# Averages of two blocks and the first dense rows turned by VectorE through DRAM, in a two-layer attention and Mish kernel

## The chip, the cores and the metric

The kernel runs on one core of a Trainium2 chip. The metric is the device time of one execution in microseconds; lower is better. The core has TensorE (PE, matrix products into PSUM), VectorE (DVE), ScalarE (ACT), GpSimd (POOL) and SyncE (SP, which issues all DMAs of this kernel in one queue).

## The reference

Two layers of the same kind over x of 2048 rows and 640 columns, all in 32 bit. Each layer is linear attention with a learned feature map, then a dense Mish block, both with a layer norm before and a residual after. The weights are the same in both layers.

```python
# attention: H = 32 heads of 20
q, k, v = heads of layernorm(x) @ wqkv
pq, pk  = q @ w_phi, k @ w_phi                     # per head
phi     = concat(softmax(p), softmax(-p))          # for q and for k, 40 features
kv, z   = phi_k^T v, sum over rows of phi_k
o       = (phi_q kv) / (phi_q z + 1e-6)            # "averages"
x       = x + o @ wo
# dense
h       = layernorm(x) @ w1 + b1                   # 640 -> 1536
x       = x + (h * tanh(softplus(h))) @ w2         # 1536 -> 640
```

## The kernel before, in words

Rows are worked on in 8 blocks (b = 0 to 7, NB = 8) of 256 rows, each of BT = 2 tiles (t = 0, 1) of 128 rows. Every large product is made of three products: an operand is split into a high part that TensorE's fast form takes, and the low rest (`xth` and `xtl` for activations, `r1h`, `r1l`, `r2h`, `r2l` for weights), and high x high, high x low and low x high are added up in PSUM.

The left operand of a product has to lie with its columns on the partitions. Rows are turned for that in one of two ways, both in the class `Transposed`:

- With `rows`: TensorE transposes 128x128 pieces against the identity (L280), ten for a block, into PSUM tiles named `one`; ScalarE copies out the high part (`xth`, recorded at L116 since all calls of the helper `act` have that line), and VectorE subtracts for the low part (`xtl`, L286).
- With `cols`: VectorE has turned the rows in 32x32 blocks (L315, `spill_turned`), eight DMAs have stored them to DRAM so that the blocks come to lie in the right place (L317, runs of 32 numbers), and `load_turned` (L325) has loaded them; `xth` and `xtl` are then made from that tile in SBUF. The dense layer uses this for its blocks 1 to 7 (`n1_d`), and the second layer's attention for its input (`n2_d`).

A layer has three stages.

1. `attend_first` makes q, k and v, the features, and the sum kv; the query features go to DRAM, turned (`e_d`).
2. `attend_second` runs over the 8 blocks. `load` (`phi`) brings the features of a block; `average` makes its averages on TensorE (L573) and VectorE divides them into a row tile `xn` (L582 to L586); they are transposed; the output projection (L344) runs in halves of 320 columns (`Rows.half`); VectorE adds the half to x in place (L603), takes the statistics (L604, L608), GpSimd makes the scale from them (L259, L260) and VectorE the shift (L262); x is stored to `x1_d` (L669). Between the blocks the dense weights are fetched (L141) and split (L148, L149, and L116). The averages run ahead of the projection: block b + 2 is averaged in the middle of block b, and block b + 1 is transposed just before it. The first dense block's rows are made in this stage as well: block 0 of `x1_d` is loaded (`fetch_dense`, L852), normalized by ScalarE (`normed`), and transposed on TensorE at the start of block 7 (`ahead.all()`, L639).
3. `dense` runs over the 8 blocks, with the first product at L695, Mish on ScalarE, VectorE and GpSimd, and the second product at L737.

What sets the order: in `attend_second` TensorE and SyncE run in exactly the order in which the code calls them (`tc.manual_schedule` on PE and SP). VectorE, ScalarE and GpSimd are ordered when the program is built, by a planner with a model of the times; afterwards each engine runs its instructions strictly in that order. A DMA with a wait holds up all DMAs behind it on SyncE's queue. Buffers come from pools of fixed counts: `big` has five tiles of 128x1280, `xn` four row tiles, `x` two blocks, and PSUM has four `one` and two `mm` tiles.

Of the kernel before, what the change touches and what calls it, by code (L numbers as in the profile page):

```python
# [8 lines left out]
F32 = mybir.dt.float32  # L9
# [33 lines left out]
def kernel(  # L43
# [58 lines left out]

    n1_d = [dram.tile([D, BLK], F32, name=f"n1_d{b}") for b in range(NB)]
    n2_d = [dram.tile([D, BLK], F32, name=f"n2_d{b}") for b in range(NB)]
    x1_d = dram.tile([S, D], F32, name="x1_d")
    x2_d = dram.tile([S, D], F32, name="x2_d")

# [157 lines left out]
    class Transposed:  # L265
# [5 lines left out]
        def step(self):  # L271
            c0 = len(self.hs)
            n = min(2, KD - c0)
            if self.rows is None:
                ps = self.cols[c0 // 2]
            else:
                ps = one_tile().rearrange("p (c s) -> p c s", c=2)
                for c in range(n):
                    for t in range(BT):
                        nc.tensor.transpose(ps[:, c, t * P:(t + 1) * P],  # L280
                                            self.rows[t][:, (c0 + c) * P:(c0 + c + 1) * P], ident)
            nb = 8 if n == 2 else 4
            hi = work.tile([P, n, BLK], F32R, tag=f"xt{n}", name="xth", bufs=nb)
            lo = work.tile([P, n, BLK], F32R, tag=f"xt{n}", name="xtl", bufs=nb)
            act(hi, ps[:, :n], AF.Copy)
            nc.vector.tensor_tensor(lo, ps[:, :n], hi.bitcast(F32), op=ALU.subtract)  # L286
            for c in range(n):
                self.hs.append(hi[:, c, :])
                self.ls.append(lo[:, c, :])
# [29 lines left out]
    def load_turned(src, tiles):  # L319

        cols = []
        for c, make in zip(range(0, KD, 2), tiles):
            n = min(2, KD - c)
            cols.append(make()[:, :n * BLK].rearrange("p (k s) -> p k s", k=n))
            nc.sync.dma_start(cols[-1], src[c * P:(c + n) * P].rearrange("(k p) s -> p k s", p=P))  # L325
        return Transposed(cols=cols)


    def project(xts, t, ws, col, ps=None):
# [220 lines left out]
                nc.vector.tensor_copy(kvb[:80, 5, :42], ps[:80, 1, :42])  # L550
        yield

    def attend_second(x_src, x_dst, acc, fetches, makes, fetch_next, begin_next):
        kva, kvz, o_ws, loaded, rest = acc
        rows = {}
        div = [None]
# [54 lines left out]
        with tc.manual_schedule(engines={mybir.EngineType.PE, mybir.EngineType.SP}):  # L611
# [21 lines left out]
            def phi(b):  # L633
                if b < NB:
                    loaded[b] = load(b)

            for b in range(NB):
                if b == NB - 1:
                    ahead.all()  # L639
# [2 lines left out]
                r0, r1 = Rows(b, 0), Rows(b, 1)  # L642
                r0.half(0, one_tile())
                tail()
                if b + 1 < NB:
                    xs[b + 1] = fetch(x_src, b + 1)
                if b in (1, 2):
                    phi(b + 3)
                if b == NB - 3:
                    fetch_next()  # L650
                r0.half(1, one_tile())
                mv0 = r0.mean()
                if b == NB - 2:
# [12 lines left out]
                r1.half(1, one_tile())  # L666
                norm_scale(b, [mv0, r1.mean()])
                xt = xs.pop(b)
                nc.sync.dma_start(row_block(x_dst, b), xt)  # L669
                makes[b]()  # L670
# [145 lines left out]
    with tc.block(schedule_with_timeline_sim=True):  # L816
        src, first = x, None
        for layer in range(LAYERS):
# [38 lines left out]
            begun = attend_second(src, x1_d, acc, [lambda s=s: fetch_step(*s) for s in steps],  # L857
                                  [lambda s=s: make_step(*s) for s in steps], fetch_dense, begin_dense)
            first = dense(x1_d, dst, w1s, w2s, [x1t[0], begun, None], last)
            src = dst  # L860

# [37 lines left out]
```

## Time and profile before

| | |
|---|---|
| time, median of 3 runs | 1398.45 us (1397.73 to 1398.70) |
| the profiled execution | 1396.09 us, its span 1394.3 us |
| TensorE busy | 1380.7 us, 99% of the span |
| VectorE / ScalarE / GpSimd busy | 1075.5 us (77%) / 583.3 us (42%) / 440.0 us (32%) |
| mean granted TensorE clock | 0.999 |
| HBM traffic | 120 GB/s over the span |

The span runs from the first to the last instruction. A row of the timeline has the start, the length, the engine, the line in the kernel, the operation, and output <- inputs by tile names (buffer numbers are left out); x10 means that ten instructions in a row are put together; a bracket names how long the engine sat idle ahead of it and what it waited for. A row of the groups has busy time, mean ns of one, and idle time before. A row of waits reads: engine, tile and line <- what it waited for: us in total, times, longest. A row of DMA issues has the count, the size and the median time from issue to landing. SPq is SyncE's queue, and its rows show how long the issue of a DMA took, not the transfer.

### The profile page before, as it was taken

How to read it: one execution, taken by the hardware profiler on the slowest of the kernel's cores; microseconds unless marked ns; L12 is line 12 of the kernel's file. 1: busy time of each engine (PE TensorE's matmuls, PEld its weight loads, DVE VectorE, ACT ScalarE, POOL GpSimd, SP SyncE). 2: the span in 40 equal slices, each digit the busy share in tenths (PEclk: the TensorE clock that was granted, in tenths of full speed). 3: DMA queues.
4: the chain of work that ended last, by engine and by line, in shares of the span. 5: the costliest groups of instructions: out<-in, count | busy, mean ns of one | idle time of the engine just before them, and what ended most of it. 6: DMA issues, size and time to landing. Idle time of an engine off the chain costs nothing. (4 is left out here: it accounts for less than half of the span.)

```text
span 1394.3 us, 28137 instructions
## 1 busy us (share of the span) xinstructions
PE 1380.7 (99%) x11528; PEld 1367.0 (98%) x11528; DVE 1075.5 (77%) x1820; ACT 583.3 (42%) x973; POOL 440.0 (32%) x334
## 2 busy tenths in 40 slices
PE   7999999999999999999999999999999999999998
PEld 7999999999999999999999999999999999999998
DVE  5797877796698877788769988888767876777775
ACT  4444433321355454545454333332235444444443
POOL 1353443343422221222234434343342211211112
PEclk9999999999999999999999999999999999999999
DMA  8533333689633432343474333357976212333200
GB/s 328 162 79 54 67 52 58 184 228 307 235 86 95 114 84 62 83 114 95 122 261 87 71 57 58 65 107 231 288 257 200 76 25 72 95 95 95 75 22 20
DMA packets 350035, 169.57 MB, mean 122 GB/s; under 512 B 286866, under 2 KB 323458, under 8 KB 349906
## 3 DMA queue, kind: packets, MB, share of 16 engines
q1 hardware_dynamic: 349906, 167.78, 44.2%
q8 instruction: 90, 1.47, 0.4%
q14 instruction: 39, 0.32, 0.1%
HBM read 104.82 MB, written 62.91 MB: 120 GB/s over the span
## 5 line engine op out<-in xcount | busy, mean ns | idle before, releaser
L737 PE MATMUL mm<-r2h,ol 128*128 128x320 f32 x1280 | 304.7, 309 | 0.0
L721 POOL TENSOR_TENSOR ol<-big,ol 128x512 fp32r<-128x512 f32 (+1 forms) x98 | 129.8, 1324 | 483.5 <-ACT ol L720 407.3
L695 PE MATMUL one<-xtl,r1h 128*128 128x256 f32 x960 | 268.2, 279 | 0.0
L695 PE MATMUL one<-xth,r1l 128*128 128x256 f32 x960 | 268.0, 279 | 0.0
L695 PE MATMUL one<-xth,r1h 128*128 128x256 f32 x960 | 265.9, 279 | 0.0
L737 PEld LDWEIGHTS mm<-r2h,ol 128*128 128x128 f32 x1280 | 219.1, 188 | 0.0
L737 PE MATMUL mm<-r2l,ol 128*128 128x320 f32 x640 | 197.3, 309 | 0.0
L344 PE MATMUL mm<-r1h,xth 128*128 128x320 f32 x600 | 187.3, 312 | 0.0
L344 PE MATMUL mm<-r1h,xtl 128*128 128x320 f32 x600 | 186.0, 310 | 0.7 <-DVE xtl L286 0.7
L344 PE MATMUL mm<-r1l,xth 128*128 128x320 f32 x600 | 186.0, 310 | 0.0
L695 PEld LDWEIGHTS one<-xtl,r1h 128*128 128x128 f32 x960 | 180.4, 188 | 0.0
L695 PEld LDWEIGHTS one<-xth,r1l 128*128 128x128 f32 x960 | 180.4, 188 | 0.0
L695 PEld LDWEIGHTS one<-xth,r1h 128*128 128x128 f32 x960 | 179.6, 188 | 0.0
L710 DVE TENSOR_SCALAR big<-big 128x512 f32<-128x512 f32 (+1 forms) x98 | 57.1, 583 | 109.9 <-ACT big L708 109.7
L379 POOL TENSOR_TENSOR r<-r,r 128x1280 f32<-128x1280 f32 x32 | 75.8, 2368 | 163.1 <-DVE r L378 157.3
L737 PEld LDWEIGHTS mm<-r2l,ol 128*128 128x128 f32 x640 | 120.2, 188 | 0.0
L712 ACT ACTIVATE big<-big,two 128x512 f32<-128x512 f32 (+1 forms) x98 | 70.1, 715 | 116.2 <-DVE big L711 116.1
L708 ACT ACTIVATE big<-one,b1s 128x256 f32<-128x256 f32 x192 | 80.8, 467 | 90.1 <-PE one L695 89.6
L720 ACT ACTIVATE ol<-big 128x512 fp32r<-128x512 f32 (+1 forms) x98 | 61.0, 622 | 136.0 <-DVE big L719 135.9
L344 PEld LDWEIGHTS mm<-r1h,xth 128*128 128x128 f32 x600 | 112.8, 188 | 1.3
L344 PEld LDWEIGHTS mm<-r1h,xtl 128*128 128x128 f32 x600 | 112.7, 188 | 1.3 <-DVE xtl L286 1.0
L344 PEld LDWEIGHTS mm<-r1l,xth 128*128 128x128 f32 x600 | 112.8, 188 | 0.1
(129 smaller groups left out, 3156.1 us busy)
## 6 DMA issues: line engine op xcount, KB each, us to landing
e_d<-r SPq DMA_DIRECT2D x128, 160.0 KB, 4.0
big<-e_d SPq DMA_DIRECT2D x32, 640.0 KB, 6.6
x_d<-xt SPq DMA_DIRECT2D x23, 640.0 KB, 3.9
xt<-x_d SPq DMA_DIRECT2D x22, 640.0 KB, 4.3
n_d<-xn SPq DMA_DIRECT2D x176, 80.0 KB, 2.1
xt<-in_x SPq DMA_DIRECT2D x16, 640.0 KB, 5.9
xn<-x_d SPq DMA_DIRECT2D x28, 320.0 KB, 4.2
v<-n_d SPq DMA_DIRECT2D x30, 256.0 KB, 3.3
```

The source lines that it names most:

```text
L344: nc.tensor.matmul(ps[:, :HC], a[:, sl], r, start=(k == 0 and n == 0), stop=(k == KD - 1 and n == 2))
L379: nc.gpsimd.tensor_tensor(eg, eg, r.unsqueeze(2).to_broadcast([P, 2 * H, DH]), op=ALU.mult)
L695: nc.tensor.matmul(ph[:, j, :], l, r, start=(n == 0), stop=(n == 3 * KD - 1))
L708: exps[0] = nc.scalar.activation(part(ta, 0)[:, j - js.start], ph[:, j, :], AF.Exp, bias=b1s[:, 2 * pr + j:2 * pr + j + 1]).ins
L710: nc.vector.tensor_scalar_min(e, e, E_CAP)
L712: nc.scalar.activation(r, n, AF.Ln, bias=two)
L720: nc.scalar.activation(ah[:, js], n, AF.Copy)
L721: nc.gpsimd.tensor_tensor(al[:, js], n, ah[:, js].bitcast(F32), op=ALU.subtract)
L737: nc.tensor.matmul(pys[t][:, c, :HC], l[:, j, sl], r, start=(f == 0 and n == 0), stop=(f == KF - 1 and n == 2))
```

## The change

The averages of blocks 6 and 7 and the rows of the first dense block no longer go through TensorE. `turn_blocks` lets VectorE turn a row tile of averages in 32x32 blocks into half of a `big` tile, `spill_blocks` stores it with eight DMAs (four for each tile, each 32 partitions with four runs of 160 numbers, 640 bytes) to a DRAM tile `o_d[b]`, and `load_blocks` loads it back in one DMA of 128 rows of 1280 numbers into another `big` tile, from which `Transposed` makes `xth` and `xtl`. The first dense block goes the way of the others, by `spill_turned` and `load_turned` with `n1_d[0]`.

The places in the loop of `attend_second`: the turns stand behind the averages of blocks 6 and 7 (in b = 4 and 5), the stores behind `norm_scale` and ahead of the store of x1, the loads of the turned blocks behind the first half of the next block (b = 5 and 6), ahead of that block's fetch of x. The load of x1's block 0 moves from b = 5 to b = 4, its normalization and turn from b = 6 to b = 5, with the store at the end of b = 5 and the load in b = 6.

In the built program these are the only differences: TensorE has 60 transposes fewer and is else the same; SyncE has the new stores and loads; ScalarE, VectorE and GpSimd differ only within blocks 4 to 7 of each layer's `attend_second`.

```diff
+    o_d = [dram.tile([P, BT * D], F32, name=f"o_d{b}") for b in range(NB)]
...
-            act(hi, ps[:, :n], AF.Copy)
-            nc.vector.tensor_tensor(lo, ps[:, :n], hi.bitcast(F32), op=ALU.subtract)
+            as_src = (lambda t: t) if len(ps.shape) == 3 else (lambda t: t.rearrange("p n (a s) -> p n a s", s=32))
+            act(as_src(hi), ps[:, :n], AF.Copy)
+            nc.vector.tensor_tensor(as_src(lo), ps[:, :n], as_src(hi).bitcast(F32), op=ALU.subtract)
...
+    def turn_blocks(o, t, dst):
+
+        nc.vector.transpose(dst[:, t * D:(t + 1) * D].rearrange("p (q c s) -> p q c s", q=4, c=KD),
+                            o.rearrange("p (c q f) -> p q c f", q=4, c=KD))
+
+    def spill_blocks(src, dst):
+        dst = dst.rearrange("(q f) (t k x) -> t k f q x", q=4, t=BT, k=4)
+        for t in range(BT):
+            for k in range(4):
+                nc.sync.dma_start(dst[t, k], src[32 * k:32 * k + 32, t * D:(t + 1) * D].rearrange("f (q x) -> f q x", q=4))
+
+    def load_blocks(src):
+        cols = big_tile()
+        nc.sync.dma_start(cols, src)
+        cols = cols.rearrange("p (a c s) -> p c a s", c=KD, s=32)
+        return Transposed(cols=[cols[:, c:min(c + 2, KD)] for c in range(0, KD, 2)])
...
+            cols, turned = {}, None
             for b in range(NB):
                 if b == NB - 1:
                     ahead.all()
...
                 r0.half(0, one_tile())
                 tail()
+                if turned is not None:
+                    cols[b + 1] = load_blocks(o_d[b + 1])
+                    turned = None
                 if b + 1 < NB:
                     xs[b + 1] = fetch(x_src, b + 1)
+                if b == NB - 2:
+                    ahead = load_next()
                 if b in (1, 2):
                     phi(b + 3)
-                if b == NB - 3:
+                if b == NB - 4:
                     fetch_next()
                 r0.half(1, one_tile())
                 mv0 = r0.mean()
-                if b == NB - 2:
-                    ahead = begin_next()
+                if b == NB - 3:
+                    spill_next = begin_next()
                 if b < 2:
                     r1.half(0, one_tile())
                 if b + 1 < NB:
-                    nxt = Transposed(rows.pop(b + 1)).all()
+                    nxt = (cols.pop(b + 1) if b + 1 in cols else Transposed(rows.pop(b + 1))).all()
                 if 2 <= b < NB - 2:
                     averages(b + 2)
                     phi(b + 4)
+                    if b + 2 >= NB - 2:
+                        turned = big_tile()
+                        for t, o in enumerate(rows.pop(b + 2)):
+                            turn_blocks(o, t, turned)
...
                 r1.half(1, one_tile())
                 norm_scale(b, [mv0, r1.mean()])
+                if turned is not None:
+                    spill_blocks(turned, o_d[b + 2])
+                if b == NB - 3:
+                    spill_next()
                 xt = xs.pop(b)
                 nc.sync.dma_start(row_block(x_dst, b), xt)
...
             def begin_dense():
-                return normed(0, x1t[0])
+                rows = [row_tile() for _ in range(BT)]
+                normalize(0, rows, [x1t[0][:, t, :] for t in range(BT)])
+                return lambda: spill_turned(rows, n1_d[0])
+
+            def load_dense():
+                return load_turned(n1_d[0], (v_tile, v_tile, row_tile))
```

More of the change, by code (lines that the diff above doesn't have):

```diff
@@ L551, in finish_kv, with attend_second @@
         yield
-    def attend_second(x_src, x_dst, acc, fetches, makes, fetch_next, begin_next):
+    def attend_second(x_src, x_dst, acc, fetches, makes, fetch_next, begin_next, load_next):
         kva, kvz, o_ws, loaded, rest = acc
@@ L854, in begin_dense @@
             def begin_dense():
-                return normed(0, x1t[0])
+                rows = [row_tile() for _ in range(BT)]
[3 more added lines that the diff above has]
+                return load_turned(n1_d[0], (v_tile, v_tile, row_tile))
             begun = attend_second(src, x1_d, acc, [lambda s=s: fetch_step(*s) for s in steps],
-                                  [lambda s=s: make_step(*s) for s in steps], fetch_dense, begin_dense)
+                                  [lambda s=s: make_step(*s) for s in steps], fetch_dense, begin_dense, load_dense)
             first = dense(x1_d, dst, w1s, w2s, [x1t[0], begun, None], last)
```

## The prediction

> **What bounds the kernel now.** I read the page's engine totals first, then TensorE's list of waits, then the chain of work that ended last around the end of the second layer's attention, and there the order of time of SyncE, ScalarE and VectorE.
>
> ```profile
> PE 1380.7 (99%) x11528; PEld 1367.0 (98%) x11528; DVE 1075.5 (77%) x1820; ACT 583.3 (42%) x973; POOL 440.0 (32%) x334
> ...
> PE mm L237 <- DMA raw<-in_wqk_t: 7.1, 3, 4.1
> PE mm L344 <- DVE xtl L286: 0.7, 1, 0.7
> ```
>
> TensorE is busy 99% of the span, and after the 7.1 us that it waits for the first weights its waits are below 1 us each. So each instruction taken from TensorE is gained, and each wait put before it is lost in full: there is no slack elsewhere.
>
> ```profile
> 1015.06 9.00 PE one L344 x60
> 1024.06 1.09 PE one L280 x10
> 1025.15 2.70 PE mm L573 x88
> 1027.85 9.00 PE one L344 x60
> 1036.84 1.09 PE one L280 x10
> 1037.93 4.59 PE one L344 x30
> 1042.52 1.09 PE one L280 x10
> 1043.61 8.80 PE one L344 x60
> 1052.41 7.58 PE one L695 x65
> ```
>
> These are start and length on that chain. L344 here is the output projection: 30 matmuls (4.4 us) are one tile of 128 rows. Blocks count from 0 to 7. Row 1015.06 is tile 1 of block 4 and tile 0 of block 5; 1024.06 the transposes of block 6's averages; 1025.15 the averages of block 7; 1027.85 tile 1 of block 5 and tile 0 of block 6; 1036.84 the transposes for block 7; 1037.93 tile 1 of block 6; 1042.52 the transposes of the first dense block's rows; 1043.61 block 7; 1052.41 the dense layer. The three transpose rows are what the change removes.
>
> **The gain.** Ten transposes hold the chain 1.09 us, and there are three such groups a layer: 3.3 us a layer, 6.5 us in all. TensorE's order is else unchanged (only these 60 instructions are missing in the built program).
>
> **What is put in their place, and where each step ends.** A block's averages now go VectorE turn, eight stores, one load, ScalarE copy, VectorE subtraction, before TensorE may use them. The first layer has the same order 676.9 us earlier, so I work the second and count it twice.
>
> ```profile
> 339.85 0.33 SPq L384 DMA_DIRECT2D xt<-in_x  x1
> ...
> 347.05 1.25 PE L280 MATMUL one<-ident,xn 128*128 128x128 f32 x10
> ...
> 1023.90 1.25 PE L280 MATMUL one<-ident,xn 128*128 128x128 f32 x10
> ```
>
> The queue of SyncE is in program order, and the new stores and loads stand among these:
>
> ```profile
> 1018.00 0.33 SPq L384 DMA_DIRECT2D xt<-x_d  x1
> 1021.03 0.33 SPq L669 DMA_DIRECT2D x_d<-xt  x1
> 1021.41 1.92 SPq L141 DMA_DIRECT2D raw<-in_w  x3
> 1025.04 0.38 SPq L384 DMA_DIRECT2D big<-x_d  x1
> 1033.41 0.38 SPq L141 DMA_DIRECT2D raw<-in_w  x1
> 1033.85 0.90 SPq L141 DMA_DIRECT2D xn<-in_w  x1
> 1062.74 4.37 SPq L317 DMA_DIRECT2D n_d<-xn  x8
> ...
> big<-x_d SPq DMA_DIRECT2D x2, 640.0 KB, 6.5
> xt<-x_d SPq DMA_DIRECT2D x22, 640.0 KB, 4.3
> n_d<-xn SPq DMA_DIRECT2D x176, 80.0 KB, 2.1
> ```
>
> ```profile
> 1030.38 0.92 ACT L116 ACTIVATE xn<-big,stats 128x640 f32<-128x640 f32 x1 [2.54 <-DMA big<-x_d]
> L116 ACT ACTIVATE xth<-v 128x512 fp32r<-128x512 f32 x30 | 17.5, 629 | 0.0
> ```
>
> ```profile
> 1018.80 0.89 DVE L586 TENSOR_TENSOR xn<-mm,den 128x480 f32<-128x480 f32 x2
> 1020.53 0.47 DVE L603 TENSOR_TENSOR xt<-one,xt 128x320 f32<-128x320 f32 x1
> 1029.71 0.89 DVE L586 TENSOR_TENSOR xn<-mm,den 128x480 f32<-128x480 f32 x2
> 1054.80 0.23 DVE L262 SCALAR_TENSOR_TENSOR stats<-mv,stats 128x1 f32<-128x1 f32 x2 [1.09 <-POOL stats L260]
> L315 DVE STREAM_TRANSPOSE xn<-xn 128x640 f32<-128x640 f32 x44 | 36.3, 834 | 2.0 <-ACT xn L116 1.9
> L286 DVE TENSOR_TENSOR xtl<-v,xth 128x512 fp32r<-128x512 f32 x30 | 21.8, 758 | 0.0
> ```
>
> *Prices.* A turn of 128x640 is not shown with a strided source; its nearest row is L315 with 0.83 us (about 0.8 in a row), and twice that is my upper end. A store of 128 runs of 640 bytes is not shown either: a 128-row load issues in 0.33 to 0.38 us, the eight stores of 640 short runs at L317 in 4.37 / 8 = 0.55; I take 0.4, nearer to the equal number of runs. They land like L317's after about 2.1 us, 4 at most. A load of 640 KB lands in 4.3 us (median of 22) to 6.5 (of 2); I take 5.3, that of the load of x1 at 1025.04, which ScalarE had at 1030.38 (1030.38 - 1025.04) with the same stores and weights ahead of it.
>
> *VectorE first.* The changed order has, behind the first turn of block 6 and its tile 1's first addition (L603), the second turn, and then the two turns of the dense rows, one each side of a bn_stats; the addition that was at 1020.53 comes after all of them. The dense rows are normalized by ScalarE from x1's first block, whose load is moved forward, to behind the load at 1018.00: issued 1018.4, landed 1023.0 by rows of 4.3 and 5.3, normalized in 0.92 each, at 1023.9 and 1024.8. So turns: 1018.80 + 0.8 (averages done) + 0.8 = 1020.4; addition 1020.9; second turn 1021.7; VectorE then waits for ScalarE until 1023.9; turn 1024.7, bn_stats 1025.1, turn 1025.9, addition 1026.4 where it was 1021.0. This wait is not TensorE's (the four "one" banks cover it), but SyncE's.
>
> *SyncE next.* The stores of block 6 leave by 1023.5. Behind them stands the store of x1's block 4, which needs that addition: 1026.5 instead of 1021.03. Then the three weight loads (1.92): 1028.9. Only then the load of the turned block 6: 1028.9 + 5.3 = 1034.2.
>
> *First wait.* ScalarE copies the first piece by 1034.85; VectorE's subtraction gives it at 1035.6, the second piece, behind a turn of block 7 (0.8) and a bn_stats (0.5), at 1037.5. Without a wait TensorE would start block 6 at 1027.85 - 1.09 + 4.4 = 1031.2. It starts 1034.85, stands again at the third chunk until 1037.5, has 8 matmuls of tile 0's first half left (1.1) and the second half (2.2), and ends tile 0 at 1040.8 instead of 1035.6. The first wait is 5.2 us. Its bounds: had the load been early, the order of VectorE alone (without the wait for ScalarE everything behind is some 2 us earlier) would hold block 6's pieces until 1032.4 and 1034.3, a wait of about 2; with the load at 6.5, x1 a microsecond later and 0.55 an issue it is 8.
>
> *Second wait.* Tile 1 of block 6 ends at 1040.8 + 4.4 = 1045.2. Block 7's second turn ends at 1036.4; before, its averages were done at 1029.71 + 0.8. Four stores go out behind it by 1038.0, the eight stores of the dense rows (4.37) by 1042.4, x1's store 1042.7, two weight loads (0.38 and 0.90) 1044.1; the load leaves there and lands at 1049.4. ScalarE 1050.0, VectorE 1050.8. TensorE starts block 7 at 1050.0 and loses another 0.5 to the subtraction: 5.3 us. Here VectorE's order sets a floor: block 7's subtractions stand behind L262 of block 6. Before the dense layer L262 started 1054.80, 2.4 after TensorE's last matmul at 1052.41; with its 0.23 and a subtraction of 0.76 the floor is 3.4. With late loads it is 8.
>
> *What else it adds, at nothing.* The turns and the subtractions from SBUF (758 ns) not counted above lie in VectorE's 23% idle time or in the waits above. The load of the dense rows leaves about 1048.5, and TensorE needs it only 9 us after block 7 starts; if that cover is gone (a landing after 1058) each microsecond counts. ScalarE's weight copies come later, but the first dense use is as much later.
>
> *Sum.* A layer: 5.2 + 5.3 - 3.3 = +7.2. Two layers: +14.4, less about 1 for the first layer, whose load ahead of x1's (339.85 + 676.9 = 1016.7) left 1.3 us earlier in the same order: +13.5. On the profiled execution of 1396.09 this gives 1409.6; the median of the runs shown is 2.4 above that execution, so 1398.45 + 13.5 = **1412**.
>
> **The rivals.** (1) *The loads are early, VectorE's order alone sets both waits*: 2 + 3.4 - 3.3 = +2.1 a layer, 1398.45 + 4 = 1402.5. For it: the 4.3 us of the common x load, and that SyncE's wait at the store of x1 is my reconstruction. Against: x1's store and weights stand ahead in the queue whatever a load takes. It decides if the load of block 6 lands before 1032.
>
> (2) *TensorE slows down after the waits.* The start of the kernel shows it: TensorE stood idle until 4.1 us and again 2.46 us,
>
> ```profile
> 10.37 2.04 PE L237 MATMUL mm<-big,raw 120*128 120x120 f32 x8 [2.46 <-DMA raw<-in_wqk_t]
> 15.29 1.59 PE L280 MATMUL one<-ident,xn 128*128 128x128 f32 x7
> ...
> 10.00:20.00 10.00, 9.63 (x51) 8.99 (x52) 7.72 (x23) 7.74 (x16) 3.08 (x6) 1.00 1.04 393
> ```
>
> and seven transposes then took 1.59 us where ten take 1.25 later: about half speed until 16.9, though the granted clock of that stretch reads 1.00. From 10.37 to 16.9 that loses half of 6.5, 3.3 us. If one wait of each layer brings it on, +6.5: 1418.5. Against: waits of 2 to 4 us may be too short, and the kernel's start may be slow for another reason. The Trainium skill, "TensorE: Matmul & The Clock Gate", Part 1, says that an idle window of about 3.4 us halves TensorE's clock and about as long a busy one restores it. By that rule both of my waits can trip it, and by the page's figure four waits would lose some 4 x 1.7 = 7 us (an estimate from that page), by the granted clock nothing; the slow rows at the start agree with the rule, the granted clock beside them does not.
>
> (3) *Everything is hidden*, the other side: the turned blocks are ready before TensorE, and the change gives its 6.5 us: 1398.45 - 6.5 = 1392. It takes block 7's subtraction before 1040, which means ahead of L262 of block 6 in VectorE's order; the order says the opposite, and only a TensorE that is late for another reason could hide it. For it stands only that the transposes surely go.
>
> **How the numbers follow.** Both waits as worked out 0.58 (1407 to 1416 by itself); rival 1 0.18; rival 2 or the long ends of loads and issues 0.18; rival 3 0.03; a mixture near no change 0.03. The long ends of both waits would be 2 x (8 + 8 - 3.3) = +25, 1424. The range 1402 to 1421 leaves out the gains, no change and the last part of the long end. What a measurement can tell from no change is about 0.2%, 2.8 us: slower 0.94, same 0.03, faster 0.03.
>
> **What will show it.** Right: TensorE's waits gain rows of 3 to 6 us at the output projection, released by ScalarE's copy or VectorE's subtraction from the turned load, two places a layer, and L280 has 60 instructions fewer. VectorE waits for ScalarE's normalized dense rows before their turns; SyncE's store of x1's block 4 waits for VectorE some 5 us longer. Wrong: the load of block 6 leaves SyncE before 1026, or the waits end at L262 rather than at a load (rival 1), or matmuls after a wait stand further apart than 0.15 us, 9.00 / 60 (rival 2).

## The result, and the profile after

The changed kernel takes 1423.06 us (median; 1421.88 to 1424.83), beside 1398.3 us for the kernel before in the same session: 1.0178 times as long, 95% interval 1.0161 to 1.0196, +24.8 us. That is slower, as forecast, and 2 us beyond the upper end of the range (1421). The profiled execution took 1424.83 us with a span of 1423.0, where the one before took 1396.09 with 1394.3; it is the span's +28.7 us that the rows below can tell of.

Line numbers have moved: L262 of before is L264 now, L286 is L289, L344 is L364, L384 is L404, L603 is L623, L695 is L729. New are L333 (the turn of the averages), L340 (their stores) and L344 (their load). In the experiments they differ by a few more; the names of the tiles stay.

Where in the span the time went shows in the first matmuls of each second pass (averages, L593) and of each dense layer (L729), from TensorE's order of time:

```profile
272.40 1.39 PE L593 MATMUL mm<-kvb,big 120*64 120x63 f32 x40
390.72 0.28 PE L729 MATMUL one<-xth,r1h 128*128 128x256 f32 x1
964.10 1.09 PE L593 MATMUL mm<-kvb,big 120*64 120x63 f32 x30
1080.91 0.28 PE L729 MATMUL one<-xth,r1h 128*128 128x256 f32 x1
```

Before, the same four stood at 271.25, 375.41, 948.18 and 1052.26. So the second pass of layer 1 went from 104.16 to 118.32 us (+14.2) and that of layer 2 from 104.08 to 116.81 (+12.7): +26.9 of the 28.7. Everything else together moved 1.8 us, 1.2 of them ahead of any changed instruction. I call these two stretches the passes below.

The page's totals and the granted clock by 40 slices (each digit tenths of full speed):

```profile
PE 1385.8 (97%) x11468; PEld 1368.6 (96%) x11468; DVE 1093.2 (77%) x1832; ACT 584.6 (41%) x973; POOL 441.4 (31%) x334
...
PEclk9999999999899999999999999999989999999999
```

TensorE has 60 instructions fewer, yet is busy 5.1 us longer, and the clock has two slices below 9, one in each pass. Its waits:

```profile
PE one L364 <- ACT xth L118: 18.8, 4, 7.1
...
PE one L364 <- DVE xtl L289: 2.8, 5, 0.9
PE one L364 <- DVE xt L623: 1.2, 2, 0.9
```

Of the rows at `one` L364 before had none: 22.8 us. The chain of layer 2's pass, where the rows of before had none but TensorE's:

```profile
1047.69 6.06 DMA big<-o_d
...
1058.17 10.29 PE one L364 x52
```

The load of the turned block 6 now stands in it, and 52 matmuls behind it take 10.29 us, 0.20 each, where 60 took 9.00 before. TensorE's rows show why:

```profile
1054.54 0.63 PE L364 MATMUL one<-r2h,xth 128*128 128x320 f32 x1 [6.10 <-ACT xth L118]
...
1056.49 0.47 PE L364 MATMUL one<-r2h,xth 128*128 128x320 f32 x1
1056.76 0.47 PE L364 MATMUL one<-r2l,xth 128*128 128x320 f32 x1
1058.17 0.63 PE L364 MATMUL one<-r2h,xtl 128*128 128x320 f32 x1 [0.95 <-DVE xtl L289]
```

After the wait matmuls follow each other by 0.27 us instead of 0.15. The windows of the same stretch (stretch, length, then busy time and count of PE, PEld, DVE, ACT, POOL, then the granted clock, DMA share, GB/s) say that this is the clock:

```profile
1052.00:1054.00 2.00, 0.00 (x0) 0.00 (x0) 0.90 (x3) 0.14 (x1) 0.00 (x0) 0.79 1.00 364
1054.00:1056.00 2.00, 1.46 (x5) 1.24 (x6) 1.48 (x3) 2.00 (x5) 0.00 (x0) 0.50 0.72 243
1062.00:1064.00 2.00, 2.00 (x11) 2.00 (x10) 0.00 (x0) 0.00 (x0) 0.30 (x1) 0.65 0.90 166
1070.00:1072.00 2.00, 0.83 (x4) 0.57 (x5) 1.16 (x4) 2.00 (x5) 0.72 (x2) 1.00 1.00 303
```

Half speed from about 1053.1, still inside the wait, to 1063.4. The second wait of this layer (2.21 us, ended at 1070.66, in the last row) left the clock alone; in layer 1 both waits halved it.

Who was late, in SyncE's queue and on ScalarE:

```profile
1035.87 0.38 SPq L404 DMA_DIRECT2D big<-x_d  x1
1036.59 5.58 SPq L340 DMA_DIRECT2D o_d<-big  x8
1045.25 0.34 SPq L703 DMA_DIRECT2D x_d<-xt  x1
...
1047.69 0.35 SPq L344 DMA_DIRECT2D big<-o_d  x1
1051.08 6.66 SPq L340 DMA_DIRECT2D o_d<-big  x8
1057.78 5.05 SPq L320 DMA_DIRECT2D n_d<-xn  x8
1062.93 0.48 SPq L703 DMA_DIRECT2D x_d<-xt  x1
...
1063.95 0.93 SPq L143 DMA_DIRECT2D xn<-in_w  x1
1064.97 0.43 SPq L344 DMA_DIRECT2D big<-o_d  x1
```

```profile
1041.93 1.73 ACT L118 ACTIVATE xn<-big,stats 128x640 f32<-128x640 f32 x2 [3.87 <-DMA big<-x_d]
1053.86 1.46 ACT L118 ACTIVATE xth<-big 128x512 fp32r<-128x512 f32 x3 [10.19 <-DMA big<-o_d]
1069.98 1.46 ACT L118 ACTIVATE xth<-big 128x512 fp32r<-128x512 f32 x3 [12.79 <-DMA big<-o_d]
```

The block 6 load leaves at 1047.69 and lands at 1053.86; block 7's leaves at 1064.97 and lands at 1069.98. And on VectorE:

```profile
1042.88 0.84 DVE L318 STREAM_TRANSPOSE xn<-xn 128x640 f32<-128x640 f32 x1 [3.73 <-ACT xn L118]
...
1044.77 0.45 DVE L623 TENSOR_TENSOR xt<-one,xt 128x320 f32<-128x320 f32 x1
...
1054.52 0.69 DVE L289 TENSOR_TENSOR xtl<-big,xth 128x512 fp32r<-128x512 f32 x1 [1.62 <-ACT xth L118]
1055.12 0.84 DVE L333 STREAM_TRANSPOSE big<-xn 128x640 f32<-128x640 f32 x1
...
1056.26 3.55 DVE L289 TENSOR_TENSOR xtl<-big,xth 128x512 fp32r<-128x512 f32 x2
```

Two things are to be seen. VectorE waits for the dense rows (3.73 us) ahead of block 4's last addition (1044.77), which x1's store at 1045.25 needs. And block 7's second turn (1055.12) stands behind the subtraction of block 6 (1054.52), which waits for block 6's load: the last four stores of block 7 cannot leave until block 6 has landed.

**The account of +26.9 in TensorE's time**: the transposes -6.5; waits at L364 +22.8; half speed some +8.8 (the clock's shortfall, 1 minus the windows' number, over the time in which TensorE worked: behind the two waits 3.2 and 1.7 in layer 1, behind the first 3.9 in layer 2); and 1.8 left over. Part of that is the matmul behind a wait: the next one starts 0.26 to 0.44 us after it instead of 0.15.

This says where TensorE's time went, and not yet what sets the end of a pass. TensorE can start block 7 only when its load has landed, and the rows show nothing ahead of that load that waits for TensorE's slow work. VectorE's second turn ends at 1055.96; from there four stores, the dense rows' stores, x1's store and two weights leave SyncE with no gap over 0.1 us until the load leaves at 1064.97, and layer 1 has the same rows without a gap. At full speed TensorE would have come to the second wait earlier and waited longer. So the half speed behind the first waits, 3.2 and 3.9 us, is taken off the second ones, and only the 1.7 us behind the second wait of layer 1 moves the end. (In layer 2 there are 0.3 us of room: block 7's first subtraction starts at 1070.99, behind L264 of block 6, and TensorE's first matmul at 1070.66.)

### The profile page after: what moved, and what is told of

Same layout as the page of the kernel before. It is cut to its first block, busy times and chain, and to the rows that moved or that the text cites. A ratio compares the mean times of both kernels' runs of the same rounds, so it can differ in the third digit from the quotient of the medians.

```text
span 1423.0 us, 28132 instructions
## 1 busy us (share of the span) xinstructions
PE 1385.8 (97%) x11468; PEld 1368.6 (96%) x11468; DVE 1093.2 (77%) x1832; ACT 584.6 (41%) x973; POOL 441.4 (31%) x334
## 5 line engine op out<-in xcount | busy, mean ns | idle before, releaser
L729 PE MATMUL one<-xtl,r1h 128*128 128x256 f32 x960 | 268.2, 279 | 0.0
L729 PE MATMUL one<-xth,r1l 128*128 128x256 f32 x960 | 268.0, 279 | 0.0
L729 PE MATMUL one<-xth,r1h 128*128 128x256 f32 x960 | 265.9, 279 | 0.0
L364 PE MATMUL mm<-r1h,xth 128*128 128x320 f32 x600 | 187.3, 312 | 0.0
L364 PE MATMUL mm<-r1h,xtl 128*128 128x320 f32 x600 | 186.0, 310 | 0.7 <-DVE xtl L289 0.7
L364 PE MATMUL mm<-r1l,xth 128*128 128x320 f32 x600 | 186.0, 310 | 0.0
L729 PEld LDWEIGHTS one<-xtl,r1h 128*128 128x128 f32 x960 | 180.4, 188 | 0.0
L729 PEld LDWEIGHTS one<-xth,r1l 128*128 128x128 f32 x960 | 180.4, 188 | 0.0
L729 PEld LDWEIGHTS one<-xth,r1h 128*128 128x128 f32 x960 | 179.6, 188 | 0.0
L364 PE MATMUL one<-r2h,xth 128*128 128x320 f32 x340 | 111.0, 326 | 20.0 <-ACT xth L118 18.8
L364 PEld LDWEIGHTS mm<-r1h,xth 128*128 128x128 f32 x600 | 112.8, 188 | 1.3
L364 PEld LDWEIGHTS mm<-r1h,xtl 128*128 128x128 f32 x600 | 112.7, 188 | 1.3 <-DVE xtl L289 1.0
```

What stands on the lines that cost most here:

```text
L364: nc.tensor.matmul(ps[:, :HC], a[:, sl], r, start=(k == 0 and n == 0), stop=(k == KD - 1 and n == 2))
L729: nc.tensor.matmul(ph[:, j, :], l, r, start=(n == 0), stop=(n == 3 * KD - 1))
```

## The experiments

The first four ask for the causes: the clock, the dense rows, the averages, the late load.

### Unneeded matmuls in the wait

```diff
+                if b >= NB - 2:
+                    idle = one_tile()
+                    for i in range(30 if b == NB - 2 else 12):
+                        nc.tensor.matmul(idle[:, :HC], o_ws[i % KD][1][:, :P], o_ws[i % KD][0][:, :HC], start=True, stop=True)
                 r0, r1 = Rows(b, 0), Rows(b, 1)
```

> The changed kernel with matmuls that are not needed put on TensorE ahead of block 6 (30) and of block 7 (12), into a PSUM tile that nobody reads, so that TensorE does not stand idle for long. Theory A (the end of each stage is set by the landing of block 7's turned load, and half speed before it is hidden by that wait): the granted clock stays at 1.00, the first wait shrinks by the 4.4 us of the added matmuls, the second wait grows by what the first stretch no longer loses, and only the half speed after the second wait of the first layer (some 2 us) is gained: about 1421. Theory B (half speed costs TensorE all that its rows lose, 11.7 us): about 1412.

Measured 1420.01 us, 1.0158 (1.0142 to 1.0174). The long waits went into the filling, but short ones stayed, and the clock still fell:

```profile
1048.77 0.41 PE L364 MATMUL one<-r2h,xth 128*128 128x320 f32 x1 [1.83 <-ACT xth L118]
```

```profile
1050.00:1052.00 2.00, 1.47 (x6) 1.06 (x4) 2.00 (x3) 1.43 (x3) 1.75 (x2) 0.50 0.40 86
```

The 84 added matmuls, 12.3 us at 0.147 each, cost nothing: +22.4 us, against +24.8 for the change. So most of the end is set by the path through DRAM, and not by what TensorE does meanwhile; and the run did not take the clock out of it as meant, since 1.83 us were enough here. It does not price the clock.

### The dense rows alone

```diff
-                    if b + 2 >= NB - 2:
+                    if False:
                         turned = big_tile()
```

> The averages of blocks 6 and 7 through TensorE as before, only the first dense block turned by VectorE. Theory A (the stores and loads of the averages are what TensorE waits for): no waits, 20 transposes gone, 2.2 us faster than before: 1396. Theory C (the dense rows' turns are what holds VectorE and all behind it): waits stay, 1403 or more.

Measured 1409.2 us, 1.0079 (1.0064 to 1.0094): slower than before, with no turned averages at all. VectorE and TensorE:

```profile
1035.17 0.84 DVE L318 STREAM_TRANSPOSE xn<-xn 128x640 f32<-128x640 f32 x1 [6.96 <-ACT xn L118]
```

```profile
1036.44 1.11 PE L282 MATMUL one<-ident,xn 128*128 128x128 f32 x4 [4.18 <-DVE xt L623]
```

VectorE stands 6.96 us at the turn of the dense rows, until ScalarE has them from x1's load. The additions behind it free the `one` tiles; four of them are soon full, and TensorE stands 4.18 us, then works at half speed (windows of 0.50 until 1043). This is theory C of the expectation. The prediction had seen the wait of VectorE and said that the four tiles cover it; here the ten transposes of block 6 use them as well.

### The averages alone

```diff
-                return lambda: spill_turned(rows, n1_d[0])
+                return normed(0, x1t[0])
```

(with the load, normalization and calls at the places of before; the 20 transposes for the dense rows are back).

> The averages turned, the first dense block through TensorE as before. Theory A: the store of x1's block 4 no longer stands behind the dense turns, so the load of block 6 leaves some 3 us earlier, and the load of block 7 without the eight dense stores some 8 us earlier; waits of about 3 and 3.5 us a layer, 40 transposes gone: 1398 + 13 - 4.4 = 1407. Theory C: no waits, 4.4 us faster than before: 1394.

Measured 1414.8 us, 1.0121 (1.0106 to 1.0136). Waits of block 6:

```profile
357.77 0.42 PE L364 MATMUL one<-r2h,xth 128*128 128x320 f32 x1 [2.61 <-ACT xth L118]
...
1045.00 0.55 PE L364 MATMUL one<-r2h,xth 128*128 128x320 f32 x1 [3.19 <-ACT xth L118]
```

against 7.07 and 6.10 in the full change: without the dense rows TensorE waits 4.5 and 2.9 us less for the load of block 6. All waits together are 13.0 us, as theory A had it; that the time is 8 us above its 1407 goes in the main to the clock, which fell to 0.50 behind the first wait of both layers here too (5.7 us by the same count as above).

### The load directly behind its stores

```diff
-                if turned is not None:
-                    cols[b + 1] = load_blocks(o_d[b + 1])
-                    turned = None
...
                     spill_blocks(turned, o_d[b + 2])
+                    cols[b + 2] = load_blocks(o_d[b + 2])
+                    turned = None
```

> The changed kernel, with the load of a turned block issued directly behind its own eight stores, ahead of the store of x1, the weight loads and the dense stores. Theory A (SyncE's queue sets when the loads leave): block 6's load leaves about 352.5 instead of 355.9 and block 7's about 364 instead of 374; waits of about 3.5 us each remain: 1406 to 1412. Theory D (the transfers themselves or VectorE's order set the waits): no change beyond 3 us, 1420 to 1424.

Measured 1419.53 us, 1.015 (1.0133 to 1.0167). The first waits shrank to 1.91 and 0.84 us, and the clock stayed at 1.00 behind them. The second ones grew:

```profile
1061.16 0.64 PE L364 MATMUL one<-r2h,xth 128*128 128x320 f32 x1 [5.27 <-ACT xth L118]
```

5.78 and 5.27 where the change has 3.45 and 2.21. The passes are +7.9 and +7.1, half of the change's; but what follows each pass is 3.2 and 4.8 us longer than before, with new waits at the dense layers' first product (2.0 for `xtl`, 1.3 for `xth`). The time lies above theory A's 1406 to 1412. So it was the place in the queue that made the first wait, and most of what it cost came back further on.

### The dense rows alone, turned later

```diff
-                nc.vector.bn_stats(self.bn[:, c], part)
+                self.last = nc.vector.bn_stats(self.bn[:, c], part).ins
...
                 if b == NB - 3:
-                    spill_next()
+                    with tc.issue_after(r1.last):
+                        spill_next()
```

on the kernel with the dense rows alone.

> The averages of all blocks go through TensorE as before; the first dense block's rows are turned by VectorE, stored and loaded as in the changed kernel, but VectorE may issue their two turns only behind the last bn_stats of block 5 (one more ordering, no other work). Theory C (in the kernel with the dense rows alone VectorE waited 4.7 and 7.0 us for ScalarE's rows ahead of additions of the same block, so no bank came free and TensorE stood for 8.8 us in all): the wait now delays additions of block 6 alone, which come 4 us later; TensorE waits for no xt, its clock stays, and with 20 transposes fewer (2.2 us) the time is about 1395.5. Rival (the wait goes where it goes, and the next additions or the later stores and load of the rows, 0.6 to 0.9 us an issue, hold TensorE at the dense layer instead): 1400 or more, with waits at L623 or at the dense layer's first matmuls.

Measured 1397.33 us, 0.9996 (0.9987 to 1.0004); 11.9 us under the same kernel without this ordering. VectorE no longer waits at the turns, and of TensorE's waits for the tiles that the additions free 0.2 us are left:

```profile
1034.49 1.55 DVE L318 STREAM_TRANSPOSE xn<-xn 128x640 f32<-128x640 f32 x2
```

Theory C holds for the dense rows by themselves: it was where the turns stood on VectorE, not the way through DRAM. The passes are 1.4 and 1.0 us shorter than before, together about the 2.2 that 20 transposes are worth; the median shows 0.4, with an interval of -1.8 to +0.6 us, since other parts of the span came out 1.4 (ahead of the first pass), 0.8 and 0.4 longer. Those I can't explain; a gain that the time shows is not established.

### The full change, dense rows turned later

The same ordering in the changed kernel.

> The changed kernel, with the two turns of the dense rows behind the last bn_stats of block 5. If the kernel with the averages alone (1414.8) and the dense rows alone when late add up, it takes about 1412.5: the load of block 6 no longer stands behind the wait for the dense rows, leaves some 3 us earlier, and the first waits fall from 7.1 and 6.1 to about 3. Rival (the wait for the dense rows only moves to where it holds block 7's stores, load and subtractions): the second waits grow by as much, and the time stays within 4 us of 1423.

Measured 1425.68 us, 1.0202 (1.0188 to 1.0216). The first waits fell as expected, to 3.14 and 3.48 us, and the second ones rose to 6.37 and 5.89: the rival. Layer 2, VectorE and SyncE:

```profile
1051.02 0.83 DVE L333 STREAM_TRANSPOSE big<-xn 128x640 f32<-128x640 f32 x1
1051.78 3.52 DVE L289 TENSOR_TENSOR xtl<-big,xth 128x512 fp32r<-128x512 f32 x2
...
1056.54 1.55 DVE L318 STREAM_TRANSPOSE xn<-xn 128x640 f32<-128x640 f32 x2
```

```profile
1063.91 0.44 SPq L344 DMA_DIRECT2D big<-o_d  x1
```

This pass began 2.2 us before the change's. Counted from its start, block 6 landed 2.3 us earlier; but the dense rows' turns now stand behind its subtractions (3.52 us for two), their stores behind the turns, and block 7's load behind the stores: it leaves 102.0 us after the start of the pass, where the change has 100.9. The pass ends when block 7's load lands, and that load hangs on a chain through VectorE and SyncE in which the first wait is only one link.

### Block 7 alone, block 6 alone

```diff
-                    if b + 2 >= NB - 2:
+                    if b + 2 == NB - 1:
```

> Only block 7's averages are turned by VectorE; block 6's and the dense rows go through TensorE as before. One wait a layer at the output projection, of block 7, of 1.5 to 3.5 us (0.5 to 1.5 of it for VectorE's subtraction), less 1.1 for ten transposes. If only the waits count: +1 to +2.5 a layer, 1399.5 to 1402.5. If a wait of this length also halves TensorE's clock for 8 us, 3.5 to 4 us of work lost: +5 to +6 a layer, 1408 to 1410.

> Only block 6's averages are turned by VectorE; block 7's and the dense rows go through TensorE as before. One wait a layer of 3 to 4.5 us (load and subtraction of block 6, as with the averages alone: 2.6 + 1.4 and 3.2 + 0.95) and half speed for 8 us behind it, 3.5 to 4 us: +6 to +7.4 a layer less 1.1, 1407.5 to 1410. Together with the kernel of block 7 alone it should give the kernel of the averages alone (+17.2) if the two waits do not work on each other; if the half speed behind the first wait hides part of the second, the two alone give more than 17.2.

(`NB - 2` in the second; the dense rows go through TensorE in both.) Measured 1402.53 us for block 7 alone, 1.0034 (1.0023 to 1.0045), and 1404.77 for block 6 alone, 1.0051 (1.0037 to 1.0064). Block 7's load left early enough to cost 0.7 us in all; 2.0 are waits for VectorE's subtraction, none over 0.6, and no window around them has the clock under 1.00. That is 2.7 us of waits against 2.2 for 20 transposes; the profiled execution took 1400.49 us, 2 under the median, so its trace does not show where the rest of the +4.8 lies. Block 6 waits 2.04 and 3.22 us, and half speed follows each, for some 3.5 and 6 us of work. Here no second wait follows to take it in: waits of 5.5, 4.7 for half speed and 2.2 less for the transposes are 8.0, and the two passes are 8.4 us longer.

The two alone give +4.8 and +7.0, 11.8 together; both at once give +17.2, so 5.4 us are what they do to each other. The dense rows add 7.6 to that at the place of the change, where alone they cost 11.6; turned later they add 10.7 (+27.9), where alone they cost nothing. So the prices of the parts do not add up, and with the late turns more than half of the loss is in none of the three parts, but in what they do to each other on VectorE and SyncE.

### Pauses put into the kernel before

```diff
+        def pause(n):
+            pt = one_tile()
+            nc.tensor.matmul(pt[:, :HC], o_ws[0][1][:, :P], o_ws[0][0][:, :HC], start=True, stop=True)
+            s = work.tile([P, 16], F32R, tag="pause", name="pause", bufs=1)
+            act(s, pt[:, :16], AF.Copy)
+            for _ in range(n):
+                act(s, s.bitcast(F32), AF.Copy)
+            nc.tensor.matmul(pt[:16, :HC], s, o_ws[0][0][:, :HC], start=True, stop=True)
```

> The kernel before with six pauses of TensorE put in by hand: ahead of blocks 1, 3 and 5 of each layer's second pass, ScalarE copies 16 columns of a PSUM tile that TensorE has just written and copies them in place 1, 4 and 8 times (first layer) and 2, 6 and 12 times (second layer), and an unneeded matmul waits for the end of it; nothing of it is used. Estimated from some 0.25 us a copy the pauses are about 1.0, 1.75, 2.75 and 1.25, 2.25, 3.75 us. The clock theory from the runs so far (waits of 0.55 to 1.0 us left the clock at 1.00; waits of 1.95 us and more mostly halved it): the pauses of 2.75 and 3.75 are followed by 3 to 10 us of half speed, those of 1.0 and 1.25 by none, those of 1.75 and 2.25 lie on the edge; time 1397.6 + 12.8 of pauses + 2 to 4 times 2 to 4 us = 1415 to 1424. Rival (an idle stretch of 3.4 us is needed): only the longest pause halves the clock, 1412 to 1414. Rival (it is not the pause but the late loads, DMA or the other engines that lower the clock): no window falls under 1.00, 1410.

Measured 1413.93 us, 1.0108 (1.0092 to 1.0125). The pauses came out shorter than estimated, 10.0 us in all: 0.52, 1.32, 2.31 in layer 1, 0.77, 1.81, 3.29 in layer 2. The third of each layer, and the windows behind it:

```profile
351.71 0.45 PE L620 MATMUL one<-r2h,pause 128*16 128x320 f32 x1 [2.31 <-ACT pause L117]
...
1009.58 0.32 PE L620 MATMUL one<-r2h,pause 128*16 128x320 f32 x1 [1.81 <-ACT pause L117]
...
1038.91 0.45 PE L620 MATMUL one<-r2h,pause 128*16 128x320 f32 x1 [3.29 <-ACT pause L117]
```

```profile
352.00:353.00 1.00, 1.00 (x5) 1.00 (x5) 0.00 (x0) 0.00 (x0) 0.00 (x0) 0.50 0.79 205
...
1009.00:1011.00 2.00, 1.42 (x10) 1.43 (x11) 0.23 (x2) 0.46 (x3) 0.88 (x2) 1.00 1.11 327
...
1042.00:1044.00 2.00, 2.00 (x10) 2.00 (x9) 0.57 (x2) 0.00 (x0) 0.00 (x0) 0.50 1.00 412
```

With none of the change's loads, stores or turns, TensorE's standing still halves its clock: in the profiled execution not after 1.81 us, but after 2.31 for 3.3 us of work, and after 3.29 for 5.6. The third reading of the expectation falls. The second falls for this execution, which was the longest of four: 1418.17 us with a mean granted clock of 0.996. The others took 1413.43 to 1414.19 us at 0.998, within the second reading's band, so half speed cost them less; which of their pauses brought it on is not known. The run shows that a stop of 2.31 us can halve the clock, not that it always does.

### GpSimd behind VectorE

```diff
+                    if from_turned:
+                        seen = work.tile([P, 1], F32, tag="seen", name="seen", bufs=2)
+                        gate = nc.gpsimd.tensor_copy(seen, nxt.ls[-1][:, :1].bitcast(F32)).ins
...
-                makes[b]()
+                if gate is not None and b < NB - 1:
+                    with tc.issue_after(gate):
+                        makes[b]()
...
```

> The changed kernel, with GpSimd's low parts of the weights behind VectorE's subtractions of the turned block (a one-column GpSimd copy of the last low part stands ahead of them; it serves nothing else). If it is GpSimd's two-input subtractions that made VectorE's subtractions from SBUF take 1.8 us instead of 0.69, they now take 0.69 each, the second stop in block 6 (0.94 and 0.95 us behind the low part) goes or falls under 0.3, and the time is 1 to 4 us under the changed kernel's 1423. Rival (they are slow because SBUF is written by the loads and stores at that moment): they stay at 1.8 and the time at 1423.

Measured 1424.93 us, 1.0188 (1.0173 to 1.0204), no gain. VectorE's rows (the second is a group: count, and shortest, median and longest in ns) did change:

```profile
1056.24 1.01 DVE L289 TENSOR_TENSOR xtl<-big,xth 128x512 fp32r<-128x512 f32 x2
```

```profile
L289 DVE TENSOR_TENSOR xtl<-v,xth x2: 693/1366/2040, 1074.0 to 1074.7; 128x512 fp32r<-128x512 f32 x2
```

In the change GpSimd's low parts of the weights ran beside block 6's subtractions:

```profile
1056.02 5.21 POOL L151 TENSOR_TENSOR r2l<-raw,r2h 128x640 fp32r<-128x640 f32 x3 [7.00 <-ACT r2h L118]
```

With them behind, the last two subtractions of block 6 take 1.01 us instead of 3.55, and the stop of 0.95 us in the middle of block 6 is gone from both layers. The second row is the other half of it: of two subtractions of the same shape for the dense rows, the one that started beside a subtraction of GpSimd's took 2.04 us, the one that started ahead of it 0.69. The time stayed because block 7's load leaves at 1064.99, as in the change: TensorE saved in block 6 what it then waited for block 7 (5.71 and 5.57 us instead of 3.45 and 2.21). TensorE starts block 7 of layer 2 at 1070.74, where the change has 1070.66. The mechanism is shown, its price in this kernel is nil; and a TensorE that gets through block 6 earlier gains nothing, since block 7's load sets the end.

### All three put apart

Late dense turns, load behind its stores, and

```diff
-                if b + 1 < NB:
+                if b + 1 < NB and not (b + 1 in cols and b == NB - 3):
                     nxt = (cols.pop(b + 1) if b + 1 in cols else Transposed(rows.pop(b + 1))).all()
...
                             turn_blocks(o, t, turned)
+                        if b == NB - 3:
+                            with tc.issue_after(last_turn[0]):
+                                nxt = cols.pop(b + 1).all()
```

> The changed kernel with three things put apart: the load of a turned block directly behind its stores, the dense rows' turns behind the last bn_stats of block 5, and VectorE's copies of block 6 behind its turn of block 7. What is left is the path itself: turn, eight stores of 0.6 to 0.9 us an issue, landing, load of 4.5 to 5, copy, some 13 us behind the averages, where TensorE comes 10 to 11 us behind them. First waits as with the early load alone (1.9 and 0.8), second waits now 1 to 2.5 instead of 5.8 and 5.3; 20 to 30 fewer us are not to be had: 1401 to 1408, the upper half if waits of about 2 us halve the clock. Rival (the second wait does not come from the first, but from the number of stores and loads in the queue): second waits of 4 to 6 remain, 1415 or more. If the loads come before TensorE needs them: 1392 to 1396, a version that beats both.

Measured 1416.85 us, 1.0132 (1.0116 to 1.0147), above the expected 1401 to 1408 and in the rival's band, though not for its reason. At the output projection it came near: waits of 0.79 and 1.71 us for block 6, 3.68 and 2.90 for block 7, passes of +4.2 and +7.5. What I had not foreseen lies behind them: what follows each pass is 4.8 and 4.4 us longer. In layer 2 VectorE's additions of block 7 wait for its rows of x,

```profile
1067.38 1.29 DVE L625 TENSOR_TENSOR xt<-one,xt 128x320 f32<-128x320 f32 x3 [5.50 <-DMA xt<-x_d]
```

whose load leaves only at 1062.05, behind the dense rows' eight stores (5.90 us), x1's store and two weights; TensorE then waits 0.69 and 1.16 us at the dense layer's first product, and the clock falls a third time (0.50 at 1072 to 1074). A version without this too was not tried.

## Why the prediction was wrong, point by point

The direction, the mechanism and the places were right; the size was low by 11 us (1412 against 1423). What was mis-sized in the main is the chain of loads and stores to block 7's load.

**The gain** came as worked out: 60 transposes are gone, and where nothing else was touched (the dense rows turned late) 20 of them gave 2.3 us in the passes.

**VectorE first.** Right in the wait, for ScalarE, of 4.28 and 3.73 us in the two layers; and in the changed kernel the four `one` tiles do cover it: VectorE's wait ends at 1042.88, and TensorE has no stop of 0.3 us or more from 1032.08 until the first wait begins at 1048.44. Without the turned averages they do not, as the dense rows alone showed (4.18 us). The 1.2 us of waits for L623 end at 339.76 and 1032.08, ahead of VectorE's wait for the dense rows, and so do not come from it.

**SyncE next.** The order was right and each link longer. Set back by the 15.9 us by which layer 2's pass began later, x1's load left at 1020.0 (predicted 1018.4), block 4's store at 1029.3 (1026.5), block 6's load at 1031.8 (1028.9) and landed at 1037.9 (1034.2); block 7's left at 1049.1 (1044.1) and landed at 1054.1 (1049.4). *The step that failed is the length of this chain*. x1's load left 1.6 us later and, taken as 4.6, needed 6.1 (7.5 in layer 1); with it came the dense rows, the additions, x1's store and block 6's load, which took 6.2 (6.6) for the 5.3 of the sum. From the end of block 7's second turn until its load left, SyncE took 9.0 us (9.4) for 7.7; the eight dense stores alone were 5.05 (5.45) for 4.37. So block 7's load landed 4.7 us later than in the sum in layer 2, and 6.5 in layer 1, where the sum less 676.9 and the 1 us for the first layer gives 371.5 and the landing, set back by 1.15, is at 378.0. The longer time was on view: in layer 1 of the kernel before, x1's load took 6.6 us (347.81 to 354.40). That the eight stores sent behind it slow x1's load in the change (291 GB/s while it was under way in layer 2, 357 before) is not shown. The stores by themselves (duration in ns, shortest, median, longest; then the time to landing):

```profile
L340 SPq DMA_DIRECT2D o_d<-big x32: 303/439/707, 344.3 to 1057.3; - x32
...
DMA to landing us min/median/max: 1.7/4.3/5.9
```

An issue is 0.44 us for the 0.4 taken (the rows above of 5.58 and 6.66 us for eight hold the wait for the second turn). They land in 4.3 us, not 2.1, but the load of block 6 left 5.5 us behind the last of its stores, so that was covered. The load of block 7 took 5.0 for 5.3, a turn with a strided source 0.84 for 0.83.

**First wait**: 5.2 predicted, 7.07 + 0.94 and 6.10 + 0.95 measured, at the bound of 8 and within it. **Second wait**: 5.3 predicted; 3.45 + 0.16 and 2.21 + 0.79 measured. It was smaller because TensorE came to it later, by the half speed (with GpSimd's work moved, TensorE came earlier and waited 5.71 and 5.57 for the same load). That block 7's load hangs on block 6's was in the sum: its 1036.4 for the second turn is 0.8 behind block 6's first subtraction at 1035.6, and the rows have that order. So block 6's lateness was carried on. The floor by L262 played almost no part, 0.3 us in layer 2. Together the waits are 22.8 us where my sum had 20 (21, less 1 for the first layer; layer 1 was in fact the worse one).

**What else it adds, at nothing**: wrong in VectorE's subtractions from SBUF. One of 128x512 takes 0.69 us by itself, and the 758 ns of the prediction is a mean over 30, half of which took 685 or less and the longest 1786; beside GpSimd's low parts of the weights it is 1.8. That made the 0.95 us inside block 6, which set no end, and the 3.01 us for block 7's three in layer 2, behind which TensorE stood 0.79.

**The step that made the miss**: in the sum's SyncE chain block 7's load landed too early, by 6.5 and 4.7 us. Of the 13.4 us by which the passes exceed my +13.5, that is 11.2; half speed behind the second wait of layer 1 is 1.7 more, and 0.5 is left.

**TensorE slows down after the waits**: rival 2 came true, and it was not in the sum. It came in three of the four places and took 8.8 us of TensorE's time (6.5 worked out), but behind the first waits it shortened the second ones, from 5.3 to 3.6 and 3.0, instead of moving the end. I argued against it that "waits of 2 to 4 us may be too short" and that the granted clock had read 1.00 at the kernel's start; but my own waits were 5 us, and the pauses show that 2.31 can be enough. By the Trainium skill, "TensorE: Matmul & The Clock Gate", Part 1, an idle window of some 3.4 us was to halve the clock. The runs agree with its two states (every window is 1.00, 0.50 or between them at a change) and differ on the length.

The prediction's long ends of both waits gave 1424, near the time measured, and that is in part luck: they had four waits of 8 us, where the runs have first ones of 8.0 and 7.1, then half speed, then second ones of 3.6 and 3.0. The other rivals fell: no load was early (1), nothing was hidden (3).

**What would show it** was seen in full: the waits at the output projection, two places a layer; 60 instructions fewer; VectorE's wait; x1's store later by 8.3 us instead of 5.5; and matmuls further apart than 0.15 us, the sign named for rival 2.

## What to carry to other kernels

When TensorE is busy 99% of the time, price a new wait with its echo: stops of 2.0 to 3.3 us were followed by half clock that cost 1.6 to 3.0 us more where no later wait took it in (block 6 alone, the pauses). Where TensorE waits for a further load behind it, that load sets the end, and it is the load's chain that has to be worked out, with the longer of the transfer times that the rows show. Moving layout work from a full engine to a path of five steps over three engines is worth its instructions only if the path ends before the old place in time: follow each step to what stands behind it in the queue of its engine, as here a turn behind a subtraction behind a load. And look at what stands behind a step that waits for a far load: by themselves the same dense rows cost 11.6 us at one place in VectorE's order and nothing at another, while in the full change the second place gained nothing, since block 7's load stood behind it.

## What the runs showed of the hardware that I had not expected

- Half clock after short stops: among single stops of 1.7 to 2.3 us, those of 1.71 (all three put apart), 1.83 (the filled kernel), 2.04 (block 6 alone) and 2.31 (the pauses) brought it on, those of 1.81 (the pauses), 1.91 (the early load) and 2.21 (the change) did not; all of 2.6 and more did. Stops of 1.0 to 1.2 us with smaller ones just ahead of them, at the dense layers of the early load and of all three put apart, did so in three of four places. It set in 2 to 5 us after TensorE stopped, in about half of the cases only when it was working again. In one-us windows each of the 29 stretches lasts 3.4, 6.8 or 10.2 us. The Trainium skill, "TensorE: Matmul & The Clock Gate", Part 1, says that the activity is watched in windows that run freely; that would give such a spread. A whole idle window of the 3.4 us that it gives can't be fitted into a stop of 2.31.
- VectorE's subtraction with both inputs in SBUF, 0.69 us for 128x512, takes 1.8 to 2.0 us while GpSimd subtracts in SBUF. The Trainium skill, "SBUF — State Buffer", section "Who interferes with whom", says so of an instruction with two SBUF inputs; the change made nine such subtractions more a layer, where before one input lay in PSUM.
